# Two attentions on one core: half pairs of exponentials, VectorE's polynomial against GpSimd's power

## The chip, the core and the metric

The kernel runs on one core of a Trainium2 chip. A core has TensorE (matrix products, into PSUM), VectorE and ScalarE (both read PSUM and the on-chip memory SBUF), GpSimd (which reads and writes SBUF, not PSUM) and a queue that issues DMA transfers. In the profile they are PE, DVE, ACT, POOL and SP. Each engine takes its instructions in order and waits on semaphores for the others. The metric is the time of one execution on the device in microseconds (us).

## The reference

Two attention layers are computed from separate inputs and put side by side: 2048 tokens, model width 576, 32 heads of 18. Layer A has one key head and one value head for all 32 query heads and no mask. Layer B has its own keys and values for each head, is causal within four segments of 512 tokens, and adds a linear memory of the segments before.

```python
def _A_ref(x, wq, wk, wv, wo):
    q = (x @ wq).reshape(B, S, H, Dh).transpose(0, 2, 1, 3)
    k, v = x @ wk, x @ wv
    scores = jnp.einsum("bhqd,bkd->bhqk", q, k) * (Dh ** -0.5)
    p = _softmax(scores, axis=-1)
    o = jnp.einsum("bhqk,bkd->bhqd", p, v)
    return o.transpose(0, 2, 1, 3).reshape(B, S, H * Dh) @ wo
# B, per segment s: a masked softmax attention a_dot of 512 x 512, a memory read
# a_mem = (phi(q) @ M) / (phi(q) @ z + 1e-6), o = g * a_mem + (1 - g) * a_dot,
# then M += phi(k)^T v and z += sum(phi(k)); at the end o @ wo
```

Everything is in 32-bit floats. The exponentials of A are the bulk of the elementwise work: 32 heads x 2048 x 2048.

## The kernel before

**Projections (to about 289 us).** Queries, keys and values of both layers are computed, split into two parts each for precision, and stored to DRAM. An upper bound of every query's scores is stored along as a shift, so that the softmax needs no running maximum: it is two further rows of the score product.

**Attention (about 289 to 1367 us).** Work goes by blocks. A block of A is one chunk of 512 queries and four heads, over 16 key tiles of 128; there are 32 blocks (4 chunks x 8 groups of heads). A block of B is one segment and four heads over 3 key steps; its 32 blocks are put in between A's in pairs, at 13 places. In each block an item is a key tile and a pair of heads (`pr` is 0 or 1): 32 items in a block of A, 6 in one of B. Items are grouped into turns of three (line 1047 on).

For an item of A, `scores` (lines 935 to 977) multiplies two heads' keys and queries into a PSUM tile `E` of 128x1024 (line 950). ScalarE takes the exponential, PSUM to the SBUF tile `P` (line 968). To give PSUM back sooner, VectorE first copies the second item of each turn into the SBUF tile `W` (line 965), and ScalarE reads that.

Some items of A are shared. For them VectorE takes the exponential of the first head of the pair, and ScalarE that of the second, out of `W`; the result lies in `PD` (two buffers) instead of `P`. The table below says which: key tile and pair, and the place in the order of products at which the item is used. The third entry is used only in blocks at whose turn no weighing step (below) is pending within four turns; `third` collects them.

```python
BY_DVE = {(0, 1): 5, (5, 0): 12, (9, 1): 15}
THIRD = (9, 1)
```

VectorE's exponential is `exponentials` (lines 920 to 933). Line 924 multiplies the scores by a constant so that their bits, written as an integer, hold the power of two in the exponent field. This comes at once, as part of the turn. Six further instructions (lines 926 to 931) separate mantissa and exponent and apply a polynomial. They go on a list, `slow`, and the main loop issues two of them in each of the following turns, two, three and four after. While the list isn't empty, `due` lets no step that costs GpSimd time begin (`heavy *= ...  and not slow`).

The products (`products`, lines 981 to 1011) follow two turns after the scores: four heads' products of `P` or `PD` with the values are accumulated in a PSUM tile `O` (line 998), which VectorE copies out at the block's end (line 1007).

GpSimd has two kinds of work in this stage. On items of B it zeroes what lies above the diagonal (line 973). And `weigh` (lines 778 to 795) multiplies finished heads by the inverse sums of their softmax; each of these is held behind VectorE's last gated instruction of the turn (`gate`), so that the engines don't meet on the memory: that is the turn's copy to `W`, or a polynomial step.

A finished chunk is projected with `wo` (line 801), in pieces of eight products that fill a place in each turn between scores and products.

The order on TensorE, ScalarE and VectorE is written out by hand; on GpSimd the weighing steps keep their order in the program, and the selects are placed where the scheduler puts them.

**The end (from about 1367 us).** The last two chunks of A are projected in a faster form that takes the whole of TensorE.

Of the kernel before, what the change touches and what calls it, by code (L numbers as in the profile page):

```python
# [8 lines left out]
F32 = mybir.dt.float32  # L9
# [3 lines left out]
U32 = mybir.dt.uint32  # L13
AF = mybir.ActivationFunctionType
ALU = mybir.AluOpType
# [34 lines left out]
LOG2 = SCALE * 1.4426950408889634  # L50
EXP_A = LOG2 * 2.0 ** 23
EXP_B = (127.0 + math.log2(0.00011720523372930181)) * 2.0 ** 23
POLY = [1.0925606709321247, 32.334180715292455, 88.7610992882796, 4291.093056129828]
MANTISSA, ONE_BITS, EXPONENT = 0x7FFFFF, 0x3F800000, 0xFF800000
# [21 lines left out]
def attention_pair_kernel(ctx, tc, a_xT, a_w, a_wo, b_xT, b_w, b_wo, b_beta, ident_d, hmask_d, bmask_d, cmask_d, sel_d, zmask_d, selx_d, sely_d, out):  # L76
    nc = tc.nc
# [79 lines left out]
    with ExitStack() as ph:  # L157
# [106 lines left out]
        for c in range(NCH):  # L264
# [34 lines left out]
            for t in TILES:  # L299
# [3 lines left out]
                else:  # L303

                    nm, bufs = ("nd", 2) if c == 1 and t == 4 else ("pj", 4)
# [25 lines left out]
                i = 5 * (c - 2) + TILES.index(t)  # L331
# [82 lines left out]
        for s in range(NSEG):  # L414
# [110 lines left out]
            if not last:  # L525
                e = p2.tile([128, 4, DH], F32, name="ph31")
# [58 lines left out]
            if s < NSEG - 1:  # L585
# [14 lines left out]
                for n, (R, ts) in enumerate(((126, slice(0, 4)), (72, slice(4, 5)))):  # L600
# [4 lines left out]
                        op=ALU.mult,  # L605
# [3 lines left out]
                for ts in (slice(0, 4), slice(4, 5)):  # L609
                    for g in range(4 if ts.start < 4 else 3):  # L610
                        rows = slice(32 * g, min(32 * g + 32, RT[ts.start]))
                        w = FIRST[ts.start == 4][g]
# [15 lines left out]
    with tc.If(loose > 0, preferred_fallthrough_block=False):  # L628
        with ExitStack() as ph:
# [37 lines left out]
            with tc.For_i(0, H, 1) as h:  # L667
# [5 lines left out]
                for i in range(NKT):  # L673
                    s, j = divmod(i, 4)
                    n = 128 * (j + 1)
# [17 lines left out]
    pp = ctx.enter_context(tc.tile_pool(name="pp", bufs=1))  # L693
# [190 lines left out]
    def run_fill():  # L884

        while fill:
            key, steps = fill[0]
            whole = next(steps, None)
            if whole is not None:
                begun.add(key)  # L890
                filled[0] += 1
                return whole
            fill.pop(0)
# [23 lines left out]
    slow, now, gate, third = [], [0], [], set()  # L917
    AFTER = mybir.DependencyInfo(mybir.DependencyClass.Sync, mybir.DependencyReason.SCHED_ONLY)

    def exponentials(p, e, whole):  # L920

        u, w = (pp.tile([128, 512], F32, name=nm, bufs=1) for nm in "nq")
        v, stt, y = nc.vector, nc.vector.scalar_tensor_tensor, p.bitcast(U32)
        v.tensor_scalar(y, e, EXP_A, EXP_B, op0=ALU.mult, op1=ALU.add)  # L924
        ops = [
            lambda: v.tensor_scalar(u.bitcast(U32), y, MANTISSA, ONE_BITS, op0=ALU.bitwise_and, op1=ALU.bitwise_or),
            lambda: v.tensor_scalar(w.bitcast(U32), y, EXPONENT, None, op0=ALU.bitwise_and),
            lambda: stt(p, u, POLY[0], u, op0=ALU.add, op1=ALU.mult),  # L928
            lambda: stt(p, p, POLY[1], u, op0=ALU.add, op1=ALU.mult),
            lambda: stt(p, p, POLY[2], p, op0=ALU.add, op1=ALU.mult),  # L930
            lambda: stt(p, p, POLY[3], w, op0=ALU.add, op1=ALU.mult),  # L931
        ]
        slow.extend((now[0] + 2 + i, p, ops[2 * i : 2 * i + 2], whole) for i in range(3))

    def scores(it, pr, copied):

# [10 lines left out]
        if ab == "A":  # L947
            for j, r0 in enumerate(HALF):
                rows = slice(r0, r0 + KR)
                nc.tensor.matmul(e[:, j], kstA[rows, 128 * kt : 128 * kt + 128], st[rows, h, :], start=True, stop=True)  # L950
            if dve:
                exponentials(p[:, 0], e[:, 0], p)
        else:
            for k, c0 in BKEYS[kt]:
                ks = slice(128 * k, 128 * k + 128)
                for j, r0 in enumerate(HALF):
                    rows = slice(r0, r0 + KR)
                    nc.tensor.matmul(  # L958
                        e[:, j, c0 : c0 + 512 - 128 * k], st[rows, 4 + h, ks], st[rows, h, 128 * k :], start=True, stop=True
                    )  # L960
# [168 lines left out]
    with tc.manual_schedule(engines={ENG.PE, ENG.Activation, ENG.DVE}):  # L1129
# [47 lines left out]
        for k in range(len(turns) + 2):  # L1177
# [4 lines left out]
            if memory is None:  # L1182
                whole = run_fill()
                while k >= len(turns) and not whole:
                    whole = run_fill()
# [163 lines left out]
```

## Time and profile before

| | |
|---|---|
| Median of the runs | 1409.2 us (two runs, 1409.04 and 1409.36) |
| Span of the profiled execution | 1404.7 us |
| Busy in it: TensorE, ScalarE | 1383.6 us, 1199.5 us |
| Busy in it: VectorE, GpSimd | 1047.3 us, 233.3 us |
| Half pairs of exponentials on VectorE | 86 |

The profile is of one execution. Its own time is the span, from the first to the last instruction; the runs' times hold 4.5 us more, which lie around it. "Busy" is the time in which an engine has at least one instruction under way. A row of a group of instructions reads: line, engine, operation, what is written <- what is read, shape, count | busy time in us, mean of one in ns | idle time of the engine just before them, and what ended it. A row of the timeline reads: start in us, duration in us, engine, line, operation, tiles, count. The chain of waits goes back from the last instruction to what released it, step by step, and gives each engine's share of the span.

### The profile page before, as it was taken

The page shows a single profiled execution, that of the slowest core. Times are in us where ns is not written, and L with a number is a line of the kernel's source. Part 1 is how long each engine was busy: PE and PEld are TensorE (multiplying, and loading weights), DVE is VectorE, ACT ScalarE, POOL GpSimd, SP SyncE. Part 2 cuts the span into 40 slices and gives each one's busy share as a digit, 9 for nine tenths or more (in the row PEclk, how much of TensorE's full clock was granted, in tenths as well). Part 3 has the DMA queues.
Part 4 walks back from the last instruction along what each step waited for, and adds up shares of the span by engine and source line. Part 5 has one row for each costly group of instructions (what it writes and reads, how often), then busy time and mean ns, then how long its engine had stood idle before and what let it go on. Part 6 is the DMA issues. An engine that isn't in the chain of part 4 may idle for free.

```text
span 1404.7 us, 41217 instructions
## 1 busy us (share of the span) xinstructions
PE 1383.6 (98%) x17452; PEld 837.7 (60%) x17452; DVE 1047.3 (75%) x1563; ACT 1199.5 (85%) x1481; POOL 233.3 (17%) x335
## 2 busy tenths in 40 slices
PE   9999999989999999999999999999999999999998
PEld 6787888745554555555555555555555555555558
DVE  6656456467787778787878878777879778887884
ACT  4543434479999999999999999999999999999991
POOL 2441000003302310412110122113010220001002
PEclk9999999999999999999999999999999999999999
DMA  9766546567575345332322452233103321120023
GB/s 283 259 213 188 168 147 216 183 175 219 151 200 180 120 139 181 95 120 85 112 59 71 133 158 60 94 104 93 51 27 94 115 75 40 31 72 21 17 68 124
DMA packets 91284, 173.63 MB, mean 124 GB/s; under 512 B 14702, under 2 KB 23015, under 8 KB 90668
## 3 DMA queue, kind: packets, MB, share of 16 engines
q1 hardware_dynamic: 84680, 160.93, 36.9%
q0 software_dynamic: 1664, 4.78, 1.3%
q10 hardware_dynamic: 4752, 5.24, 1.2%
q8 instruction: 138, 2.26, 0.7%
q14 instruction: 50, 0.41, 0.1%
HBM read 99.65 MB, written 70.67 MB: 121 GB/s over the span
## 4 chain that ended last, share of the span: by engine, by line
PE 64%; ACT 6%; DVE 4%; issue 2%; DMA 1%; POOL 0%; SPq 0%; POOLq 0%; DVEq 0%; ACTq 0%
PE O L998 31%; PE E L950 19%; PE F L801 11%; ACT P L968 6%; PE E L958 3%; DVE W L965 2%; PE F L857 1%; DMA o<-oA 0%; DVE sm L750 0%; DVE PD L930 0%; DVE PD L928 0%; POOL o L785 0%; DMA rb<-rA 0%; DMA o<-o 0%; DVE o L862 0%
## 5 line engine op out<-in xcount | busy, mean ns | idle before, releaser
L968 ACT ACTIVATE P<-E 128x1024 f32<-128x1024 f32 (+1 forms) x800 | 787.6, 1076 | 4.4 <-PE E L950 4.2
L965 DVE COPY W<-E 128x1024 f32<-128x1024 f32 (+2 forms) x416 | 453.3, 1090 | 145.2 <-PE E L950 83.9
L998 PE MATMUL O<-P,VA 128*32 128x256 f32 x7504 | 507.6, 380 | 0.0
L968 ACT ACTIVATE P<-W 128x1024 f32<-128x1024 f32 (+1 forms) x330 | 369.9, 1121 | 6.1 <-DVE W L965 5.6
L998 PEld LDWEIGHTS O<-P,VA 128*32 128x32 f32 x7504 | 259.8, 110 | 138.0 <-issue 6.1
L950 PE MATMUL E<-stA,kstA 56*128 56x512 f32 x1920 | 317.0, 430 | 2.0 <-ACT P L968 1.8
L950 PEld LDWEIGHTS E<-stA,kstA 56*128 56x128 f32 x1920 | 155.3, 184 | 158.3 <-issue 94.2
L973 POOL TENSOR_SCALAR_AFFINE_SELECT P<-P 128x256 f32<-128x256 f32 (+1 forms) x192 | 94.6, 493 | 414.7 <-ACT P L968 376.7
L785 POOL TENSOR_TENSOR o<-o,rb 126x512 f32<-126x512 f32 (+1 forms) x55 | 72.8, 1348 | 431.1 <-DVE PD L931 185.1
L801 PE MATMUL F<-woB,o 126*32 126x192 f32 (+1 forms) x1920 | 126.6, 338 | 0.0
L998 PE MATMUL O<-PD,VA 128*32 128x256 f32 x688 | 88.9, 379 | 0.0
L801 PEld LDWEIGHTS F<-woB,o 126*32 126x32 f32 (+1 forms) x1920 | 38.7, 108 | 74.9 <-issue 69.6
L998 PE MATMUL O<-P,vseg 128*32 128x256 f32 (+2 forms) x1536 | 81.4, 344 | 0.1
L924 DVE TENSOR_SCALAR PD<-E 128x512 uint32<-128x512 f32 x86 | 59.2, 689 | 23.5 <-PE E L950 21.7
L1007 DVE COPY oe<-O 128x512 f32<-128x512 f32 x64 | 44.3, 692 | 42.4 <-PE O L998 39.8
L253 PE MATMUL pj<-xh,wBh 128*126 128x512 f32 x180 | 72.2, 401 | 0.0
L253 PE MATMUL pj<-xh,wBl 128*126 128x512 f32 x180 | 71.7, 398 | 0.0
L122 ACT CAST qp<-pj 126x512 fp32r<-126x512 f32 (+1 forms) x54 | 31.0, 584 | 44.2 <-DVE kmB L459 27.8
L123 DVE TENSOR_TENSOR qp<-pj,qp 126x512 fp32r<-126x512 f32 (+1 forms) x54 | 36.8, 686 | 37.8 <-ACT qp L122 37.8
L801 PE MATMUL F<-woA,o 126*32 126x192 f32 (+1 forms) x960 | 64.0, 338 | 0.0
L958 PE MATMUL E<-stB 56*128 56x256 f32 (+3 forms) x512 | 61.6, 348 | 2.1 <-ACT P L968 1.3
L998 PEld LDWEIGHTS O<-P,vseg 128*32 128x32 f32 x1536 | 49.0, 110 | 24.3 <-issue 1.9
(206 smaller groups left out, 1573.2 us busy)
## 6 DMA issues: line engine op xcount, KB each, us to landing
stB<-kB SPq DMA_DIRECT2D x96, 144.0 KB
stB<-qB SPq DMA_DIRECT2D x32, 288.0 KB
stA<-qA SPq DMA_DIRECT2D x30, 288.0 KB
oA<-oe SPq DMA_DIRECT2D x32, 256.0 KB
oB<-oe SPq DMA_DIRECT2D x32, 256.0 KB
qA<-qp SPq DMA_DIRECT2D x16, 504.0 KB
kB<-qp SPq DMA_DIRECT2D x16, 504.0 KB
qB<-qp SPq DMA_DIRECT2D x16, 504.0 KB
```

The lines of the kernel that those rows point to most:

```text
L123: hold(nc.vector.tensor_tensor(qp[:R, 1, :n], src, qp[:R, 0, :n].bitcast(F32), op=ALU.subtract))
L253: nc.tensor.matmul(dst, w[:, c0 : c0 + M], x, start=i == 0, stop=i == len(ops) - 1)
L785: ins = tc.keep_in_program_order(nc.gpsimd.tensor_tensor(dst, a, b, op=op))
L801: nc.tensor.matmul(dst[32 * j : 32 * j + 32], parts[ab, c][: RT[t], t, r0 : r0 + 32], wo[ab][: RT[t], t, c0 : c0 + n], start=start, stop=stop,
L924: v.tensor_scalar(y, e, EXP_A, EXP_B, op0=ALU.mult, op1=ALU.add)
L950: nc.tensor.matmul(e[:, j], kstA[rows, 128 * kt : 128 * kt + 128], st[rows, h, :], start=True, stop=True)
L958: nc.tensor.matmul(e[:, j, c0 : c0 + 512 - 128 * k], st[rows, 4 + h, ks], st[rows, h, 128 * k :], start=True, stop=True)
L965: gate.append(nc.vector.tensor_copy(src[:, hs, :n], e[:, hs, :n]))
L968: nc.scalar.activation(p[:, hs, :n], src[:, hs, :n], AF.Exp, scale=SCALE)
L973: nc.gpsimd.affine_select(diag, diag, pattern=[[0, 2], [0, m], [1, 128]], base=0, channel_multiplier=-1, compare_op=ALU.is_ge, fill=0.0)
L998: nc.tensor.matmul(o[32 * j : 32 * j + 32, q0 : q0 + n], v, p[:, j % 2, p0 : p0 + n], start=m == hf == 0, stop=last and hf == 1,)
L1007: nc.vector.tensor_copy(osb, o)
```

## The change

`exponentials` no longer takes the exponential on VectorE. VectorE multiplies the scores by `LOG2` (the softmax's scale times the logarithm of e to base 2), from PSUM to `PD` as floats. One GpSimd instruction then raises a tile of twos to these powers, in place. It is issued at once, in the turn of the scores, and keeps its place in the program's order beside the weighing steps. The tile of twos lies where one of the two helper tiles was and is filled once. `slow` stays empty, so the main loop's steps on it never run, and `due` is no longer held back by it. The table of shared items and their places in the products' order is as before.

```diff
@@ -917,20 +917,13 @@
     slow, now, gate, third = [], [0], [], set()
     AFTER = mybir.DependencyInfo(mybir.DependencyClass.Sync, mybir.DependencyReason.SCHED_ONLY)
 
+    two = pp.tile([128, 512], F32, name="n", bufs=1)
+    nc.gpsimd.memset(two, 2.0)
+
     def exponentials(p, e, whole):
 
-        u, w = (pp.tile([128, 512], F32, name=nm, bufs=1) for nm in "nq")
-        v, stt, y = nc.vector, nc.vector.scalar_tensor_tensor, p.bitcast(U32)
-        v.tensor_scalar(y, e, EXP_A, EXP_B, op0=ALU.mult, op1=ALU.add)
-        ops = [
-            lambda: v.tensor_scalar(u.bitcast(U32), y, MANTISSA, ONE_BITS, op0=ALU.bitwise_and, op1=ALU.bitwise_or),
-            lambda: v.tensor_scalar(w.bitcast(U32), y, EXPONENT, None, op0=ALU.bitwise_and),
-            lambda: stt(p, u, POLY[0], u, op0=ALU.add, op1=ALU.mult),
-            lambda: stt(p, p, POLY[1], u, op0=ALU.add, op1=ALU.mult),
-            lambda: stt(p, p, POLY[2], p, op0=ALU.add, op1=ALU.mult),
-            lambda: stt(p, p, POLY[3], w, op0=ALU.add, op1=ALU.mult),
-        ]
-        slow.extend((now[0] + 2 + i, p, ops[2 * i : 2 * i + 2], whole) for i in range(3))
+        nc.vector.tensor_scalar(p, e, LOG2, None, op0=ALU.mult)
+        tc.keep_in_program_order(nc.gpsimd.tensor_tensor(p, two, p, op=ALU.pow))
 
     def scores(it, pr, copied):
```

## The prediction

> **What bounds the kernel now.** I read the busy shares and the chain of waits first, then the busy time in the stretch in which half pairs exist, then the timeline of a few turns.
>
> ```profile
> span 1404.7 us, 41217 instructions
> ...
> PE 1383.6 (98%) x17452; PEld 837.7 (60%) x17452; DVE 1047.3 (75%) x1563; ACT 1199.5 (85%) x1481; POOL 233.3 (17%) x335
> ...
> PE 64%; ACT 6%; DVE 4%; issue 2%; DMA 1%; POOL 0%; SPq 0%; POOLq 0%; DVEq 0%; ACTq 0%
> ```
>
> The profiled execution took 1404.7 us inside its span; the median of the runs is 1409.2, so 4.5 us lie around the span, and I add them to every sum. Nearly two thirds of the chain is TensorE's; VectorE, which the change relieves, has 4% of it (56 us), GpSimd nothing.
>
> The window view, over the attention stage and then from the end of the first half pair's scaling to the start of the last product that reads one:
>
> ```profile
> core 0: us, PE busy (x) PEld busy (x) DVE busy (x) ACT busy (x) POOL busy (x), PEclk, DMA share, GB/s
> 310.00:1340.00 1030.00, 1025.29 (x14739) 555.33 (x14742) 824.62 (x1149) 1022.76 (x1169) 176.92 (x260) 1.00 0.33 100
> 289.80:1366.60 1076.80, 1070.41 (x15344) 579.10 (x15347) 863.93 (x1206) 1067.88 (x1221) 177.07 (x261) 1.00 0.33 101
> ```
>
> In 1030 us TensorE is idle for 4.7, ScalarE for 7.2; VectorE has 205 us free, GpSimd 853. Busy may hide a stretched matmul, so here are TensorE and VectorE in two neighbouring turns:
>
> ```profile
> 719.94 0.97 PE L950 MATMUL E<-stA,kstA 56*128 56x512 f32 x6
> ...
> 720.72 0.69 DVE L924 TENSOR_SCALAR PD<-E 128x512 uint32<-128x512 f32 x1
> ...
> 722.60 0.95 PE L950 MATMUL E<-stA,kstA 56*128 56x512 f32 x6
> ...
> 723.49 0.53 PE L801 MATMUL F<-woB,o 126*32 126x192 f32 x8
> ...
> 723.84 1.48 PE L998 MATMUL O<-P,VA 128*32 128x256 f32 x24
> ...
> 725.25 0.97 PE L950 MATMUL E<-stA,kstA 56*128 56x512 f32 x6
> ```
>
> The turn with a half pair in it (719.94 to 722.60) takes 2.66 us, the one without (722.60 to 725.25) 2.65. ScalarE has half an activation less to do in the first and VectorE an exponential more, and neither shows: scores (0.89), projection (0.35) and products (1.41) follow each other without a gap and fill the turn. In this stage TensorE sets the pace.
>
> **What the change removes.** The groups of the six polynomial steps, of the scaling, and of the two GpSimd operations that I use as prices:
>
> ```profile
> L924 DVE TENSOR_SCALAR PD<-E 128x512 uint32<-128x512 f32 x86 | 59.2, 689 | 23.5 <-PE E L950 21.7
> L926 DVE TENSOR_SCALAR n<-PD 128x512 uint32<-128x512 uint32 x86 | 35.9, 417 | 0.0
> L927 DVE TENSOR_SCALAR q<-PD 128x512 uint32<-128x512 uint32 x86 | 36.2, 422 | 0.0
> L928 DVE SCALAR_TENSOR_TENSOR PD<-n 128x512 f32<-128x512 f32 x86 | 58.7, 682 | 0.0
> L929 DVE SCALAR_TENSOR_TENSOR PD<-PD,n 128x512 f32<-128x512 f32 x86 | 59.5, 692 | 3.0
> L930 DVE SCALAR_TENSOR_TENSOR PD<-PD 128x512 f32<-128x512 f32 x86 | 58.6, 682 | 0.0
> L931 DVE SCALAR_TENSOR_TENSOR PD<-PD,q 128x512 f32<-128x512 f32 x86 | 59.5, 692 | 3.0
> L785 POOL TENSOR_TENSOR o<-o,rb 126x512 f32<-126x512 f32 x44 | 59.0, 1362 | 286.9 <-DVE PD L931 185.1 <-DMA o<-oA 98.8 <-DVE W L965 2.4
> L973 POOL TENSOR_SCALAR_AFFINE_SELECT P<-P 128x512 f32<-128x512 f32 x64 | 40.8, 637 | 12.0 <-ACT P L968 8.1 <-PE E L958 0.5 <-PE O L998 0.3
> ```
>
> The six steps at lines 926 to 931 sum to 308 us of VectorE and go. The new scaling reads the same 128x512 out of PSUM at the same place as line 924, so I price it as that row, 0.69 us, and it costs nothing more. What the 308 us are worth is bounded by TensorE's 4.7 us of idle time in the stage: the copies to W would no longer stand behind polynomial steps, but what is late next is TensorE itself. I take a gain of 4 us. Nothing is its lower bound, since fewer instructions on an engine that doesn't set the pace can't lengthen it; the upper one is TensorE's idle time in the longer stretch, 6.4 us, and as much again for small stalls that busy matmuls may hide, 13.
>
> **What it adds.** One power of two on GpSimd for each half pair, 86 of them: 32 blocks of A with two each, and 22 of the blocks with a third. With the list of slow steps always empty, the weighing steps are no longer held back in the turns behind a half pair, so blocks may find nothing pending more often and take their third; the bounds are 86 and 96, and I count 88. ScalarE's saving by two further half pairs is nothing, by the two turns above.
>
> The new wait: the power waits for VectorE's scaling, the products wait for the power. Products stand in order on TensorE, and behind a late one stand the next scores, hence everything. On GpSimd, the selects of B's diagonals and the weighing steps stand behind a power. The time that a power has is seen in one block, from its three scalings to the products that read them, with the next block's first scaling last:
>
> ```profile
> 713.19 0.69 DVE L924 TENSOR_SCALAR PD<-E 128x512 uint32<-128x512 f32 x1
> ...
> 726.94 0.39 PE L998 MATMUL O<-PD,VA 128*32 128x256 f32 x2
> ...
> 728.67 0.69 DVE L924 TENSOR_SCALAR PD<-E 128x512 uint32<-128x512 f32 x1
> ...
> 739.50 0.39 PE L998 MATMUL O<-PD,VA 128*32 128x256 f32 x2
> ...
> 744.82 0.38 PE L998 MATMUL O<-PD,VA 128*32 128x256 f32 x2
> ...
> 741.68 0.69 DVE L924 TENSOR_SCALAR PD<-E 128x512 uint32<-128x512 f32 x1 [1.12 <-PE E L950]
> ```
>
> The first, scaled by 713.88, has 13.1 us; the second (720.72, shown above), 18.1; the third, 15.5. Alone, a power of 13 us is hidden. In a row they are not: this block, three powers, lasts 28.5 us from scaling to scaling, so at over **9.5 us** each GpSimd falls further behind with each such block. Over the whole stretch the limit is (1076.8 - 177.1) / 86 = **10.5 us**. Below it, this change is free; above it, every microsecond of the power costs 86.
>
> The tile of twos is filled once, ahead of the stage, on an engine that is idle there: nothing. The weighing steps now wait only for a copy to W of their turn (within 2.65 us) and hold back a power by no more, which 13 us cover.
>
> The trace has no power. From below, the nearest row is the plain two-input operation of the same length, 1.36 us. From above I price it by its arithmetic. The exponential that VectorE did is two one-input steps and four two-input steps after the scaling; at GpSimd's rows (0.637 and 1.362) that is 6.7 us. But the base comes in as a tensor of twos, and an operation that takes any base has to find its logarithm first; with as many steps again it is 13.4 us. Steps for signs, zeros and overflow may double that, 26.9. Against these stands that the steps inside one operation are not instructions of their own, and the trace doesn't tell how much of the two rows a step in the middle would pay. I take 13.4, the price of the full arithmetic at rows of this very engine, rather than 1.36, a row that does one multiplication; both ends stay in the range.
>
> The sum at 13.4: GpSimd must do 86 x 13.4 + 177 = 1330 us in a stretch of 1077, so the stretch grows by 253, and the end comes at 1404.7 + 253 + 4.5 = 1662; two further half pairs make it 1689. I say **1690**. At 26.9 it is 86 x 26.9 + 177 - 1077 = 1413 more, **2822**.
>
> [...]
>
> **Rivals.** *The power fits.* Its place is GpSimd's free time (853 us of the stage), its decision point 9.5 us, and then the time is 1404.7 - 4 + 4.5 = **1405**, between 1396 (a gain of 13) and 1412 (a late power here and there). For it: the slack above, and that 6.7 us, an exponential without the logarithm, is already under the point. Against it: that takes an operation made for this base. [...]
>
> *Selects behind powers.* GpSimd works in order, so a select on B's diagonal can stand behind the power of A's next block, in a power of any length:
>
> ```profile
> 704.72 0.42 POOL L973 TENSOR_SCALAR_AFFINE_SELECT P<-P 128x256 f32<-128x256 f32 x1 [28.97 <-ACT P L968]
> ...
> 708.89 1.37 PE L998 MATMUL O<-P,vseg 128*32 128x256 f32 x24
> ```
>
> This one ends at 705.14, and its product starts at 708.89, so it has 3.7 us. B's heads are put between A's blocks in 13 groups, so a power of 6.7 us that got ahead of the last selects of each would cost 13 x (6.7 - 3.7) = 39 us: 1405 + 39 = **1444**; it decides from a power of about 4 us on. Against it: the last selects belong to the turn before the one whose scores feed the power, and need nothing from it.
>
> *A power far over 27 us*, if the operation handles each element by a long sequence that overlaps nothing. At 40 us (three times 13.4) the sum is 86 x 40.2 + 177 - 1077 = 2557 more, **3966**. Only the absence of any such row speaks of it, either way; it is the forecast's mechanism with another price.
>
> That the change doesn't do what it says I give no chance: the six steps are in no list any more, and nothing else raises two to a power.
>
> **How the numbers follow.** GpSimd becomes the bound, with a power between 10.5 and 27 us: 0.43, forecast 1690, its own range 1412 to 2822. The power fits: 0.35. Selects behind powers: 0.05. A power beyond 27 us: 0.17. I hold the bound likelier than the fit (0.60 to 0.35) because the arithmetic of a general power at GpSimd's rows lies above the point of 9.5 us and only half of it, or the row of a bare multiplication, lies below. The range takes in the fit, the selects and the bound up to its upper end, and leaves out the 0.17 above: 1396 to 2822. A measurement of this kernel tells about 2% from no change, 28 us. Faster by that would need half of VectorE's 56 us on the chain to be real time though TensorE has 6.4 us to give: 0.02. Within it: the fit without that, 0.33. Slower: 0.43 + 0.17 + 0.05 = 0.65.
>
> **What the profile after would show.** The mean of the new GpSimd group against 9.5 us decides nearly all. If I am right, GpSimd is busy for nearly the whole stretch, the chain of waits goes through it, TensorE's waits before products that read PD name GpSimd, and VectorE and ScalarE show idle time that they didn't have; the stretch's growth divided by the number of powers gives the power less 10.5. If the power fits, turns stay at 2.65 us, GpSimd's busy time grows by the number of powers times their mean, and no wait of TensorE's names it. VectorE's busy time should fall by 308 us in either case, and the scaling stay at 0.69; a scaling that takes longer, or copies to W that start no earlier, would show my reading of VectorE wrong. The number of powers, 86 to 96, tests the reading of the thirds. A time outside both cases, such as 1430 with powers of 3 us, would say that something else stands in GpSimd's queue, the selects or a weighing step that waits for a transfer.

## The result, and the profile after

The changed kernel takes 7794.7 us, against 1409.2 before: a ratio of 5.535 with a 95% interval of 5.524 to 5.545. The forecast was 1690, its range 1396 to 2822.

The page of the changed kernel, the span, the busy shares and the chain by engine:

```profile
span 7794.2 us, 40974 instructions
...
PE 1615.8 (21%) x17452; PEld 906.9 (12%) x17452; DVE 771.1 (10%) x1049; ACT 1221.5 (16%) x1481; POOL 7456.8 (96%) x424
...
issue 57%; POOL 37%; PE 2%; ACT 0%; DVE 0%; DMA 0%; POOLq 0%; DVEq 0%; SPq 0%; ACTq 0%
```

GpSimd was busy for 17% and is now for 96%; every other engine is idle most of the time. ("issue" in the chain is time for which the profile shows no releaser. It is 57%, and GpSimd is idle for only 4% of the span, so GpSimd runs through most of it.) The groups that carry the time are the power, the scaling ahead of it and the products behind it; behind `exponentials`, line numbers are 7 lower than before:

```profile
L926 POOL TENSOR_TENSOR PD<-n,PD 128x512 f32<-128x512 f32 x88 | 7227.8, 82154 | 3.7 <-DVE PD L925 3.6
...
L991 PE MATMUL O<-PD,VA 128*32 128x256 f32 x704 | 168.5, 632 | 6088.5 <-POOL PD L926 6088.5
...
L925 DVE TENSOR_SCALAR PD<-E 128x512 f32<-128x512 f32 x88 | 60.9, 692 | 3062.2 <-PE E L943 3062.0
```

One power takes **82.15 us**. There are 88 of them, and TensorE sits idle for 6088 us in front of products that wait for one. The wait view (us in total, number of waits, longest) says the same, and shows where GpSimd itself waited:

```profile
PE O L991 <- POOL PD L926: 6088.5, 87, 75.7
...
POOL P L966 <- ACT P L961: 56.8, 99, 2.3
```

The window view of the stretch from the first power's start to the last one's end (columns as in the prediction's window view):

```profile
290.50:7753.20 7462.70, 1299.06 (x15343) 645.77 (x15340) 591.70 (x691) 1091.75 (x1224) 7399.53 (x350) 0.58 0.05 15
```

The stretch was 1077 us before and is 7463. The 88 powers take 88 x 82.154 = 7230 of it, which leaves 233.

On the chips of the experiments the kernel before took 1406.7 to 1407.5 in the comparisons, and ratios below are to runs of it beside them. One execution of the run "The weighing steps alone", 1676.6 us at a granted clock of 0.75 against 0.99 or more in its other ten, is left out of its ratio.

### The profile page after: what moved, and what is told of

It reads as the page before. It is cut to its first block, busy times and chain, and to the rows that moved or that the text cites. A ratio compares the mean times of both kernels' runs of the same rounds, so it can differ in the third digit from the quotient of the medians.

```text
span 7794.2 us, 40974 instructions
## 1 busy us (share of the span) xinstructions
PE 1615.8 (21%) x17452; PEld 906.9 (12%) x17452; DVE 771.1 (10%) x1049; ACT 1221.5 (16%) x1481; POOL 7456.8 (96%) x424
## 4 chain that ended last, share of the span: by engine, by line
issue 57%; POOL 37%; PE 2%; ACT 0%; DVE 0%; DMA 0%; POOLq 0%; DVEq 0%; SPq 0%; ACTq 0%
POOL PD L926 36%; PE O L991 1%; POOL o L785 1%; PE E L951 1%; PE E L1241 0%; ACT P L961 0%; PE F L801 0%; POOL rb L785 0%; DVE PD L925 0%; DVE oe L1000 0%; DMA rb<-rB 0%; DMA rb<-rA 0%; PE E L943 0%; PE O L1241 0%; PE F L1241 0%
## 5 line engine op out<-in xcount | busy, mean ns | idle before, releaser
L926 POOL TENSOR_TENSOR PD<-n,PD 128x512 f32<-128x512 f32 x88 | 7227.8, 82154 | 3.7 <-DVE PD L925 3.6
L961 ACT ACTIVATE P<-E 128x1024 f32<-128x1024 f32 (+1 forms) x800 | 761.4, 1010 | 6226.3 <-PE E L943 4472.0
L991 PE MATMUL O<-PD,VA 128*32 128x256 f32 x704 | 168.5, 632 | 6088.5 <-POOL PD L926 6088.5
L991 PEld LDWEIGHTS O<-PD,VA 128*32 128x32 f32 x704 | 49.0, 159 | 6168.6 <-POOL PD L926 6127.4
L991 PE MATMUL O<-P,VA 128*32 128x256 f32 x7488 | 613.8, 423 | 0.0
L925 DVE TENSOR_SCALAR PD<-E 128x512 f32<-128x512 f32 x88 | 60.9, 692 | 3062.2 <-PE E L943 3062.0
L943 PE MATMUL E<-stA,kstA 56*128 56x512 f32 x1920 | 352.0, 474 | 0.0
L961 ACT ACTIVATE P<-W 128x1024 f32<-128x1024 f32 (+1 forms) x328 | 345.9, 1055 | 5.0 <-DVE W L958 2.0
L943 PEld LDWEIGHTS E<-stA,kstA 56*128 56x128 f32 x1920 | 175.5, 209 | 174.5 <-issue 102.6
L244 POOL TENSOR_TENSOR wBl<-wr,wBh 128x648 fp32r<-128x648 f32 (+2 forms) x15 | 22.1, 1476 | 44.1 <-ACT wBh L243 26.6
```

What stands on the lines that cost most here:

```text
L925: nc.vector.tensor_scalar(p, e, LOG2, None, op0=ALU.mult)
L926: tc.keep_in_program_order(nc.gpsimd.tensor_tensor(p, two, p, op=ALU.pow))
L961: nc.scalar.activation(p[:, hs, :n], src[:, hs, :n], AF.Exp, scale=SCALE)
L991: nc.tensor.matmul(o[32 * j : 32 * j + 32, q0 : q0 + n], v, p[:, j % 2, p0 : p0 + n], start=m == hf == 0, stop=last and hf == 1,)
```

## Experiments

**One multiplication in place of the power.** All of the change stays except what the operation computes.

```diff
-        tc.keep_in_program_order(nc.gpsimd.tensor_tensor(p, two, p, op=ALU.pow))
+        tc.keep_in_program_order(nc.gpsimd.tensor_tensor(p, two, p, op=ALU.mult))
```

> The power is replaced by one multiplication by the tile of twos; the exponential of the half pairs is left out. Everything else of the change stays: the scaling on VectorE, the new wait, GpSimd's order. Theory (the power's own length is the whole cost, and TensorE sets the pace once it is gone): 88 operations of about 1.36 us on GpSimd, no wait of TensorE's names them, time 1405, between 1396 and 1412. Rival (the new wait and the order on GpSimd cost time by themselves, selects or weighing steps standing behind it): above 1420. Second rival (VectorE's polynomial did hold the kernel back): below 1381, 28 us of the 56 on the chain.

Measured: 1400.0, ratio 0.9948 (0.9934 to 0.9962). Chain and attention stage of this run:

```profile
PE 72%; ACT 3%; issue 2%; DVE 1%; DMA 1%; SPq 0%; POOL 0%; POOLq 0%; DVEq 0%; ACTq 0%
```

```profile
310.00:1340.00 1030.00, 1027.70 (x14854) 557.25 (x14850) 572.40 (x672) 1027.72 (x1176) 285.11 (x344) 1.00 0.33 101
```

The new wait, the order on GpSimd and the empty list of slow steps cost nothing. With VectorE relieved of 252 us in this window (824.6 before) the kernel is 7 us faster, 0.5%: VectorE's share of the chain falls from 4% to 1%, TensorE's rises from 64% to 72%. Both rivals fall.

**Six, eight and ten multiplications.** The same operation, repeated, makes GpSimd's work as long as one likes, at 1.36 us a piece.

```diff
-        tc.keep_in_program_order(nc.gpsimd.tensor_tensor(p, two, p, op=ALU.pow))
+        for _ in range(6):  # or 8, or 10
+            tc.keep_in_program_order(nc.gpsimd.tensor_tensor(p, two, p, op=ALU.mult))
```

> Six multiplications in a row in place of the power (the exponential of the half pairs is left out): 6 x 1.36 = 8.2 us of GpSimd for each half pair, below the 9.5 us at which a block of three would overrun. Theory: 1405, like one multiplication, within 5 us. Rival (selects stand behind it): 13 places at 8.2 - 3.7 us, 1405 + 58 = 1463.

> Ten multiplications (the exponential of the half pairs is left out): 13.6 us for each of 88 half pairs, over the limit. Theory: 88 x 13.6 + 177 - 1077 = 297 us more than 1409, 1706. Rival (GpSimd's time doesn't add up in this simple way, because TensorE, ScalarE and GpSimd each wait in turn): well above, 1409 plus 88 x (13.6 - 4) = 2250 if nothing of it overlaps the slack; if the slack of 13 to 18 us per power covers it: 1405.

Measured: six, 1400.4, ratio 0.9950 (0.9934 to 0.9965), the same as one. Ten, 1753.9, ratio 1.246 (1.244 to 1.249). So 8.1 us of GpSimd for each half pair are free, and 13.5 are not, as the slack said; at 8.1 us the selects behind them cost nothing, where the rival put 1463. But the sum for ten was 48 us short. The timeline of GpSimd and the window over its stretch in the run with ten:

```profile
650.41 13.49 POOL L927 TENSOR_TENSOR PD<-n,PD 128x512 f32<-128x512 f32 x10
...
666.44 13.53 POOL L927 TENSOR_TENSOR PD<-n,PD 128x512 f32<-128x512 f32 x10
```

```profile
291.40:1713.30 1421.90, 1168.28 (x15343) 603.68 (x15340) 595.55 (x691) 1086.08 (x1224) 1296.71 (x1142) 0.90 0.26 77
```

88 x 13.51 = 1189 of 1422 leaves 233, the same rest as with the power, where my sum put 177, GpSimd's other busy time. The difference is about the time in which GpSimd, though it sets the pace, waits for ScalarE between B's selects: 57 us by the wait row of the changed kernel above. Eight multiplications test the 233:

> Eight multiplications in place of the power (the exponential of the half pairs is left out), 10.8 us by the spacing of 1.36 us in the run with ten. If GpSimd's other work in the stretch costs the 233 us that the runs with ten multiplications and with the power both leave (with its waits for ScalarE between B's selects): 88 x 10.8 + 233 - 1077 = 106 us over 1407, 1513. With the 177 us of its busy time alone: 50 over, 1457.

Measured: 1509.9, ratio 1.073 (1.071 to 1.075), 3 us from the sum with 233 and 53 from the one with 177. The limit of the whole stretch is therefore (1077 - 233) / 88 = 9.6 us for a half pair, not 10.5. This is worked out; no run lies between 8.1 and 10.8.

**What the power's time depends on.** Single operations behind the end of the kernel before, on constant tiles (`x` 1.5, base 2 unless said otherwise):

```diff
+        pin(g.tensor_tensor(y, base, half, op=ALU.pow))
+        pin(g.tensor_tensor(y[:, :256], base[:, :256], half[:, :256], op=ALU.pow))
+        pin(g.tensor_tensor(y[:, :64], base[:, :64], half[:, :64], op=ALU.pow))
+        pin(g.tensor_tensor(y[:16], base[:16], half[:16], op=ALU.pow))
+        pin(g.tensor_tensor(y[:1], base[:1], half[:1], op=ALU.pow))
...
+        pin(g.tensor_scalar(y, half, 2.0, None, op0=ALU.mult))
+        pin(g.tensor_scalar(y, half, 1.25, 3.5, op0=ALU.mult, op1=ALU.add))
...
```

> The kernel before, whole, with a row of GpSimd operations behind its end, read one by one from the trace: the power of 128x512, 128x256, 128x64, 16x512 and 1x512; 128x512 with exponents 1.5, 0, -20.3 and -200 and with base 1; a multiplication and one-input operations beside them. If the power is a fixed sequence for each column: 82 us, 41, 10.3, and 82 for 16 rows and for one, the same for all values. [...] If it branches on values: the exponent 0, the base 1 and the underflow at -200 take less. If most of it is a fixed start (code loading): 128x64 takes far over 10.3.

The timeline of GpSimd (start, duration):

```profile
1393.65 82.22 POOL L1301 TENSOR_TENSOR P<-W,P 128x512 f32<-128x512 f32 x1
1475.94 41.23 POOL L1302 TENSOR_TENSOR P<-W,P 128x256 f32<-128x256 f32 x1
1517.26 10.55 POOL L1303 TENSOR_TENSOR P<-W,P 128x64 f32<-128x64 f32 x1
1527.88 82.13 POOL L1304 TENSOR_TENSOR P<-W,P 16x512 f32<-16x512 f32 x1
1610.08 82.13 POOL L1305 TENSOR_TENSOR P<-W,P 1x512 f32<-1x512 f32 x1
1692.29 82.15 POOL L1306 TENSOR_TENSOR P<-W,P 128x512 f32<-128x512 f32 x1
...
1856.75 1.52 POOL L1308 TENSOR_SCALAR P<-P 128x512 f32<-128x512 f32 x1
1858.35 0.62 POOL L1309 TENSOR_SCALAR P<-P 128x512 f32<-128x512 f32 x1
...
1860.64 82.17 POOL L1312 TENSOR_TENSOR P<-W,P 128x512 f32<-128x512 f32 x1
...
1943.47 82.14 POOL L1314 TENSOR_TENSOR P<-W,P 128x512 f32<-128x512 f32 x1
...
2026.28 82.14 POOL L1316 TENSOR_TENSOR P<-W,P 128x512 f32<-128x512 f32 x1
```

From 64 to 512 columns the time grows by (82.22 - 10.55) / 448 = **160 ns a column**, with about 0.3 us of start. The number of rows makes no difference, 1, 16 or 128; nor do the values: the exponent 0 (line 1306), -200, -20.3 (lines 1312 and 1314) and the base 1 (line 1316) take the same, and so do the scores of the changed kernel (82.15). The time goes by columns alone, as the first theory has it; branching on these values and a costly start fall. What the operation does in the 160 ns, no run shows.

**The power, over 32 columns only.**

```diff
-        tc.keep_in_program_order(nc.gpsimd.tensor_tensor(p, two, p, op=ALU.pow))
+        tc.keep_in_program_order(nc.gpsimd.tensor_tensor(p[:, :32], two[:, :32], p[:, :32], op=ALU.pow))
```

> The power over 32 of the 512 columns (the others are left without their exponential): by 160 ns for a column 5.1 to 5.5 us. Theory (only the length of the power matters): 1400, as with one multiplication. Rival (a power holds up other engines while it runs, as by the memory that it reads): above 1407.

Measured: 1399.5, ratio 0.9946 (0.9928 to 0.9964), with powers of 5.43 us:

```profile
L926 POOL TENSOR_TENSOR PD<-n,PD 128x32 f32<-128x32 f32 x88 | 477.7, 5429 | 214.7 <-DVE PD L925 125.3 <-ACT P L961 88.2 <-DMA stB<-qB 0.6
```

The power of 5.4 us is as free as one multiplication (1399.5 us against 1400.0): it takes no time from the other engines that the kernel's time would show.

**The weighing steps alone.** The kernel before, with the one other thing that the change does to the order of work:

```diff
-        heavy *= "B" not in near and not slow
+        heavy *= "B" not in near
```

> The kernel before, with one thing of the change alone: the list of slow steps no longer holds back the weighing steps. VectorE keeps its polynomial. If the 0.5% that one multiplication gave comes from VectorE's relief: no change, 1407 within 0.2%. If it comes from the weighing steps' new places: 1400.

Measured: 1407.5, ratio 1.0005 (0.9996 to 1.0014). The 0.5% of the multiplication is not from the weighing steps, nor from the two further half pairs, since this kernel has 88 as well. VectorE's relief is what is left of the change: an argument by elimination.

**The polynomial on GpSimd.** At 8.1 us for a half pair GpSimd's time was free, up to 9.6 it should be by the limit worked out above, and VectorE's relief is worth up to 0.5%. So the four polynomial steps, a sum and a product each, might move there, with the whole result kept:

```diff
+        def step(dst, a, c, b):
+            tc.keep_in_program_order(nc.gpsimd.tensor_scalar(dst, a, c, None, op0=ALU.add))
+            tc.keep_in_program_order(nc.gpsimd.tensor_tensor(q if b is not p else p, dst, b, op=ALU.mult))
...
+            step(q, u, POLY[0], u)
+            step(q, q, POLY[1], u)
+            step(u, q, POLY[2], q)
+            step(q, q, POLY[3], p)
```

> The whole computation, as in the kernel before, with the four polynomial steps of each half pair moved to GpSimd, each as an addition of a constant and a multiplication; the scaling and the two bit operations stay on VectorE. By the rows, 4 x (0.62 + 1.36) = 7.9 us of GpSimd for each half pair, below 9.5, and 236 of the 308 us taken off VectorE. Theory (relief of VectorE is worth 0.5%, and arithmetic on GpSimd below the limit costs nothing): between 1400 and 1403, against 1407 before. Rival (GpSimd's and VectorE's operations on the on-chip memory hold each other up, or the additions are dearer, as the 1.52 us of the first one): 88 x 11.5 + 233 - 1077 = 168 us more, 1575.

Measured: 1618.8, ratio 1.151 (1.150 to 1.153): the rival, for the most part by GpSimd's own additions.

```profile
L927 POOL TENSOR_SCALAR q<-q 128x512 f32<-128x512 f32 x176 | 275.2, 1563 | 15.4
```

An addition of a constant alone takes 1.56 us here, about as long as the constant product of line 1308 above (1.52), while a product and a sum in one instruction (line 1309) took 0.62. By this run's rows a half pair is four additions of 1.54 us on average, four products of 1.28 and eight gaps of 0.08, together 11.92, and 88 x 11.92 + 233 - 1077 = 205 over 1407 is 1612, 7 us short of the measured time. With the faster form it is the next run:

```diff
-            tc.keep_in_program_order(nc.gpsimd.tensor_scalar(dst, a, c, None, op0=ALU.add))
+            tc.keep_in_program_order(nc.gpsimd.tensor_scalar(dst, a, 1.0, c, op0=ALU.mult, op1=ALU.add))
```

> The whole computation, the four polynomial steps on GpSimd as in the run that gave 1619, but each addition is written as a multiplication by one and an addition in one instruction, the form that took 0.62 us in the row of single operations, against 1.52 for one operation alone. GpSimd then needs 4 x (0.69 + 1.36) = 8.2 us for a half pair. Theory (the length of GpSimd's work was all that was wrong): 1400 to 1403. Rival (the helper tile that GpSimd holds makes VectorE wait and its copies to W late): 1420 or more, with VectorE's bit operation waiting for GpSimd.

Measured: 1415.4, ratio 1.0058 (1.0044 to 1.0072). The additions of the row below fell to 0.64 us and most of the loss with them, but it isn't faster. The rows of this run:

```profile
L927 POOL TENSOR_SCALAR q<-q 128x512 f32<-128x512 f32 x176 | 112.2, 638 | 15.4
...
L931 DVE TENSOR_SCALAR PD<-PD 128x512 uint32<-128x512 uint32 x88 | 77.2, 878 | 3.0
```

```profile
DVE n L939 <- POOL q L928: 11.3, 4, 5.2
...
PEld E L959 <- DVE W L974: 10.8, 10, 4.1
```

VectorE waits for the helper tile that GpSimd still reads, copies to W come late behind that, and TensorE's scores behind them: 11 us. And the bit operation of line 931, 0.42 us before, takes 0.88 on average. That average hides two cases, of which the timeline of this run shows one each:

```profile
338.70 0.43 DVE L931 TENSOR_SCALAR PD<-PD 128x512 uint32<-128x512 uint32 x1
...
724.25 1.40 POOL L928 TENSOR_TENSOR PD<-q,PD 128x512 f32<-128x512 f32 x1
724.53 1.40 DVE L931 TENSOR_SCALAR PD<-PD 128x512 uint32<-128x512 uint32 x1
```

Of the 88, 38 take 0.43 us, and none of these overlaps an operation of GpSimd with two input tiles. 37 take 1.4 us, and every one of them overlaps such an operation by 1.1 us or more; the one of 724.53 ends 0.28 us after the multiplication that it started in. The other 13 take 0.72 and overlap the first 0.2 us of one. So it is not that the operation now writes in place, which all 88 do.

Only the last two steps on GpSimd, with the weighing steps not held back (which alone changed nothing, above):

```diff
+        def step(c, b):
+            tc.keep_in_program_order(nc.gpsimd.tensor_scalar(u, p, 1.0, c, op0=ALU.mult, op1=ALU.add))
+            tc.keep_in_program_order(nc.gpsimd.tensor_tensor(p, u, b, op=ALU.mult))
...
+            step(POLY[2], p)
+            step(POLY[3], w)
```

> The whole computation, with the last two of the four polynomial steps on GpSimd (2 x 2.05 = 4.1 us for a half pair) and the weighing steps not held back; 119 of the 308 us are taken off VectorE. If VectorE's relief is what gives the 0.5%: between 1401 and 1406; if GpSimd's part comes late for the first half pair's slack of 13 us: above 1410.

Measured: 1462.0, ratio 1.039 (1.038 to 1.041), slower than either. Here the helper tile is written by VectorE early and held until GpSimd is done, and the wait view shows GpSimd and VectorE waiting for each other over it, with TensorE's scores late behind VectorE's copies:

```profile
POOL n L926 <- DVE PD L930: 273.3, 62, 11.5
...
DVE n L936 <- POOL PD L927: 109.4, 52, 3.1
...
PE E L958 <- DVE W L973: 40.8, 33, 2.9
```

No product of TensorE's waits for GpSimd in this run, so the slack of 13 us in front of the products, the second branch above, isn't what it ran out of; the time is above 1410 by another way. The worth of VectorE's relief is thus not in question in this run; a hand-over between two engines through one buffer is.

A second buffer for the tile, with the steps on GpSimd as before it:

```diff
-        u, q = (pp.tile([128, 512], F32, name=nm, bufs=1) for nm in "nq")
+        u, q = (pp.tile([128, 512], F32, name=nm, bufs=b) for nm, b in (("n", 2), ("q", 1)))
...
-            osb = pa.tile([128, C], F32, name="oe", bufs=4)
+            osb = pa.tile([128, C], F32, name="oe", bufs=3)
```

> The whole computation, as in the run that gave 1415, with a second buffer for the helper tile that VectorE's bit operation writes and GpSimd reads (paid for by one buffer less for the outputs on their way to DRAM). If VectorE's waits for that tile, and the copies to W behind them, were what kept it from the 1400 of the multiplications: 1400 to 1403. If it is GpSimd's length near the limit (8.2 us with three half pairs in 28.5), or the memory that the two engines share: 1410 to 1416 again.

> The same with the weighing steps not held back by the list of slow steps, so that GpSimd's queue is that of the runs with multiplications, step for step. If the order on GpSimd is what differs from them: 1400; if the second buffer or the shared memory decides: as the run beside it, within 2 us.

Measured: 1408.9, ratio 1.0014 (1.0005 to 1.0023), and with the weighing steps freed 1409.0, ratio 1.0012 (1.0003 to 1.0021). The buffer gave back most of what was lost; the order on GpSimd made no difference. The result is within 0.2% of the kernel before, not better. In the first of the two, VectorE's bit operation still takes 0.90 us on average:

```profile
L931 DVE TENSOR_SCALAR PD<-PD 128x512 uint32<-128x512 uint32 x88 | 78.9, 897 | 3.0
```

Why these two don't reach the 1400 of six multiplications, which keep GpSimd nearly as long, stays open: they have two VectorE bit operations more for each half pair, one of them at 0.90 us on average, and one output buffer less, and the runs don't tell these apart. So no run that computes the whole result shows the 0.5%; only those that leave the exponential out do.

## Why the prediction was wrong

The mechanism and its place were right, and the limit nearly; the size of one term was off by a factor of six.

- **The price of the power** is the step that failed. I built it from GpSimd's rows for single instructions, two one-input and four two-input steps, doubled for the logarithm to 13.4 us, and set the upper end at twice that, 26.9. It measures 82.15, 160 ns for each of 512 columns. Nothing in the trace of before bounds it from above: rows of plain instructions say what their arithmetic costs, not how long another operation takes. The steps for a logarithm, signs, zeros and overflow were my estimate: no run shows them or the upper end of 26.9 that they gave, only the 160 ns a column. I named the row of a bare multiplication as the lower bound, and that stands; the upper bound was a guess dressed as a sum, and the rival "far over 27 us", at 0.17, is what happened, at twice the 40 us that I priced it with. (The upper end was also summed with 86 powers, though I counted 88; with 88 it is 2876, still far too low.) The mistake in the chances was to hold an unseen operation within a factor of two of a construction.
- **The sum.** With the measured power and 88 of them, as I had counted, it gives 1404.7 + 88 x 82.154 + 177 - 1077 + 4.5 = 7739. With 233 for GpSimd's other work in place of 177 it gives 7795, and the measured time is 7794.7. The 233 is read from this very run, but the run with ten multiplications gives the same, and the one with eight was forecast by it to 3 us. The 56 us between the two are, by the wait row, GpSimd waiting for ScalarE between B's selects, which I had taken as time that a power would fill.
- **The limit.** 9.5 us in a block of three and 10.5 over the stretch were forecast; 8.1 us cost nothing, 10.8 cost 103 us and 13.5 cost 347, so that the stretch's limit is 9.6. That the decision point of 9.5 lies so near is partly luck: it came from a block of three, and the sum over the stretch, which sets the limit, was 0.9 us too wide.
- **TensorE as the bound before**: right. One multiplication in place of the power gives 0.5%, 7 us, where I took 4 and at most 13. Had the power fitted, the time would have been within 2% of the kernel before, as the rival said: it put 1405 beside 1409, and the run with one multiplication took 1400 beside 1407.
- **VectorE's relief.** The busy time fell by 276 us, from 1047.3 to 771.1, not by 308. The six groups' busy times, added up, count twice where one instruction's row overlaps the next one's: in the timeline of before the copy behind the scaling of 720.72, which lasts 0.69, starts at 721.33, 0.08 us before that one's end. The scaling stayed at 0.69.
- **Thirds.** 88 half pairs, as counted: two more blocks than before took their third.
- **Selects behind powers**: no, at a length of 8.1 us on GpSimd; the time was that of one multiplication.

## What to carry to other kernels

An operation that no profile has shown has no upper price: "one instruction in place of six" says nothing of time, and here the one took 82 us. Measure such an operation by itself, over two sizes, before a kernel is built on it; here one look at 64 and 512 columns would have told 160 ns a column against a slack of 13 us. The slack itself, and the sum of an engine's work over the stretch, can be read from the profile to a few microseconds; count the engine's waits inside the stretch with its work.

## What the runs showed of the hardware

- GpSimd's power took 82.13 to 82.22 us over 512 columns, with 128, 16 and 1 rows and with each of the values tried, and 10.55 over 64: 160 ns a column. A whole 128x512 multiplication took 1.28 us on average in the run with one in place of the power.
- On GpSimd one operation with a constant took 1.49 to 1.56 us over 128x512, by the means of the groups in the run that took 1619 us and the single operation (1.52); two in one instruction took 0.62 to 0.72, by those in the run that took 1415 and the single one (0.62).
- In the run that took 1415 us, VectorE's bit operation of line 931, SBUF to SBUF, took 0.43 us in the 38 of 88 that overlapped no GpSimd operation with two input tiles, and 1.4 us in the 37 that overlapped one by 1.1 us or more. That GpSimd's operation holds VectorE's up is read from this overlap; by what, no run shows.
- In the changed kernel TensorE came out of a wait of 69 us slow. Right after that wait and some microseconds later:

```profile
372.75 0.64 PE L991 MATMUL O<-PD,VA 128*32 128x256 f32 x2 [68.93 <-POOL PD L926]
...
374.60 1.65 PE L943 MATMUL E<-st,kstA 56*128 56x512 f32 x6
...
378.84 0.96 PE L943 MATMUL E<-st,kstA 56*128 56x512 f32 x6
```

Six score matmuls took 1.65 us and 4 us later 0.96; the granted clock was 0.50 from 372.00 to 376.30 and 1.00 from 378.80 to 381.00. Over the whole stretch it was 0.58, against 1.00 before, and the products of `PD` took 632 ns on average, against 379. It shows in no sum: what the powers leave of the stretch is 233 us here and 233 with ten multiplications, at a clock of 0.90.
